# Layer two's spatial mixing: two of seven block products divided once more, their matrix sums made by DRAM transfers, and one gate a step

## The chip, the core and the metric

One core of a Trainium2 chip runs the whole program. The metric is the device time in microseconds of one execution; the kernel before took 1393.39 us (median of 3 runs, 1393.29 to 1393.97). Engines are named as the profile names them: PE (TensorE, matmuls), PEld (its weight loads), DVE (VectorE), ACT (ScalarE), POOL (GpSimd) and SP (SyncE, which only issues DMAs here).

## The reference

Four residual blocks on x, 2048 tokens by 512: linear attention, gated MLP, and both once more with the same weights. What the change touches is the gated MLP's mixing over tokens:

```python
z = _gelu(jnp.einsum("bsd,df->bsf", x, w_in))      # 2048 x 1792
z1 = z[..., :Fh]                                   # Fh = 896
z2 = _layernorm(z[..., Fh:], axis=-1)
g = jnp.einsum("ts,bsf->btf", w_sp, z2) + b_sp[None, :, None]   # w_sp: 2048 x 2048
return jnp.einsum("bsf,fd->bsd", z1 * g, w_out)
```

`w_sp` z2 is a product of 2048 x 2048 by 2048 x 896, once in each of the two layers, in float32.

## The kernel before

Every float32 matmul is made as three float32r ones: each operand is split into a high part (ScalarE copies it to float32r, `high`, L106, or L838 and L868 in the mixing) and the residual (VectorE subtracts, `low`, L109, or L839, L870 and L872), and the products high·high, high·low and low·high go to one PSUM bank (`mm3`, L120 to L122; in the mixing `acc`, L900 to L902). All engines run in the order in which the program issues their instructions; the programmer writes this order by hand.

A layer is class `P1` (attention's projections and its K-V sums, 17 steps), `transition`, class `P2` (attention's output, and the MLP's input projections; step by step for 16 tiles of 128 tokens, and with the transposed product for z1 in `f`, L673, whose GELU results go to DRAM), and class `P4`: the mixing (g = 0 to 55) and then the output projection (`o`, L988, 16 tiles of 128 tokens). During layer one's output tiles `join` (L1048) begins layer two: it loads x and weights, computes statistics and splits weights.

The mixing treats `w_sp` as 2 x 2 blocks (1024 x 1024) and z2 as 2 x 2 blocks (1024 tokens; features H1 = 0 to 383 and H2 = 512 to 895, while H3 = 384 to 511 is done in the plain way). Seven block products in the order P2, P1, P6, P7, P4, P5, P3 (`ORDER`, L808) take the place of eight. Each has 8 steps `(p, k)`, one for each 128 rows of the inner dimension. A step has six groups of three matmuls (2 row blocks of 512 tokens by three 128-feature blocks), and in P1, P2, P4 and P5 two more for H3 (`WITH3`). All matmuls are 128 x 128 by 128 x 512. P6 and P7 go on in the banks of the product before them; P2, P1 and P5 take fresh ones.

Of `w_sp`, P1, P2 and P4 read blocks of it (512 KB a step); the others read sums of blocks, made once in layer one by class `Sums` (GpSimd additions, L780, one `tick` a step) and kept in DRAM for both layers.

The loop of `P4.run` (L1013) does at iteration g: `fetch(g + 4)` (the DMA of the raw weights, issued by SP), `sp(g + 2)` (splits the weights, L838 and L839; forms the z operand, L846 to L866, and splits it, L868 to L872), `mm(g)` (the matmuls), and at a product's last step `evac` (L930: VectorE adds the bank to the result, or to the bias of the token, L937 to L960), which in four products then queues all the product's gates at once (`gate`, L924: GpSimd multiplies a 128 x 512 result by its z1 tile). z1 is loaded in one go for each of these products (`loadz1`, L907). Where P6 ends, the evacuation goes ahead of the next split, as P7 goes on in the same banks. Buffers are taken from slot lists, oldest free one first: 6 `quads` (raw weights take one, split weights one), 22 `pages`, 8 PSUM `banks`. A weight split at g thus waits for the matmuls of g - 3, and a load for the split of the raw weights three steps back.

Of the kernel before, what the change touches and what calls it, by code (L numbers as in the profile page):

```python
# [29 lines left out]
class Slots:  # L30
# [16 lines left out]
    def put(self, *tiles):  # L47
        for t in tiles:
            n, _ = self.held.pop(id(t))
            self.free_list.append(n)  # L50


@with_exitstack
def mixer_kernel(ctx: ExitStack, tc: tile.TileContext, x_in, wqkv, wo_d, win1_d, win2_d, wsp_d, bsp_d, wout_d,
# [198 lines left out]
    class P1:  # L253
# [180 lines left out]
        def run(self, sums):  # L434
            side = deque([self.win2] * NF)
            ND = NT - DEFER
            for s in range(1, NT + 2):
# [29 lines left out]
                if s == 6:  # L467
                    self.wv, self.wo = (quads.get([P, 4, 512]) for _ in range(2))
                    nc.sync.dma_start(self.wv, wqkv[:, 1024:1536].rearrange("(c p) f -> p c f", p=P))
                    nc.sync.dma_start(self.wo, wo_d.rearrange("(c p) f -> p c f", p=P))  # L470
                if s > 3 and side:
                    side.popleft().piece()
# [66 lines left out]
    class P2:  # L539
# [152 lines left out]
        def run(self, sums):  # L692
            w1 = self.win1
            for s in range(1, NT + 3):
# [52 lines left out]
                if s > 4:  # L747
                    sums.tick()
                if s >= NT + 1:
                    self.p4.fetch(s - NT - 1)  # L750
# [4 lines left out]
    class Sums:  # L755
# [3 lines left out]
        def __init__(self):  # L759
# [4 lines left out]
            self.slots = pages  # L764

        def fetch(self):
            if self.ahead:
                k, j, h = self.ahead.popleft()
                at = ((j, k), (j, k + HT), (2 + j, k)) if h == 0 else ((2 + j, k + HT),)
                self.raw.setdefault((k, j), []).extend(load(wsp_d[n, s], self.slots) for n, s in at)  # L770

# [32 lines left out]
    class P4:  # L804
# [5 lines left out]
        H1, H3, H2 = slice(0, 384), slice(384, 512), slice(512, 896)  # L810

        def __init__(self, p2, sums):
# [3 lines left out]
            self.steps = [(p, k) for p in self.ORDER for k in range(HT)]  # L816
            self.beta = self.delta = None
            self.wout = {}

        def fetch(self, g):  # L820
# [4 lines left out]
            if p in ("P1", "P2", "P4"):  # L825
# [6 lines left out]
        def sp(self, g):  # L832
            if g >= len(self.steps):
                return
            p, k = self.steps[g]
# [5 lines left out]
            self.w[g] = w  # L841
            H1, H2, H3 = self.H1, self.H2, self.H3
# [6 lines left out]
            elif p == "P1":  # L849
                z = a[:, 0:512]  # L850
                nc.vector.tensor_add(a[:, H2], a[:, H2], b[:, H2])
# [4 lines left out]
            else:  # L856
                tmp = pages.get(PAGE)
                z = tmp[:, 0:n]
                if p == "P7":
                    nc.vector.tensor_sub(z, a[:, H2], a[:, H1])  # L860
                elif p == "P4":
# [15 lines left out]

        def mm(self, g):
            p, k = self.steps[g]
            h, l = self.z.pop(g)  # L880
            w = self.w.pop(g)
            first, last = k == 0, k == HT - 1
            if p in ("P2", "P4") and first:
# [3 lines left out]
            if p in self.WITH3:  # L887
                for j in range(2):
                    self.acc(self.delta[j], h, l, self.H3, w, j, first and p in ("P2", "P4"),
# [6 lines left out]
            quads.put(w)  # L896

# [9 lines left out]
        def loadz1(self, p):  # L907
            js = range(2)
            todo = {"P1": [(2 + j, 3) for j in js] + [(2 + j, f) for j in js for f in range(3)],
                    "P4": [(j, f) for j in js for f in range(3)],  # L910
                    "P5": [(j, 3) for j in js] + [(j, 4 + f) for j in js for f in range(3)],
                    "P3": [(2 + j, 4 + f) for j in js for f in range(3)]}
            for n, f in todo.get(p, ()):
# [200 lines left out]
```

## Time and profile before

| | |
|---|---|
| median of 3 runs | 1393.39 us |
| the profiled execution | 1393.49 us |
| its span, first to last instruction | 1391.6 us |
| DVE, ACT, POOL busy in the span | 853.8, 562.1, 387.7 us |
| layer two's mixing in the span | about 1039.5 to 1311 us |

A profile has: the page (busy times, 40 slices, DMA queues, the chain that ended last, groups of instructions); lists of who waited for whom; timelines (start, duration, engine, line, operation, output and inputs; in brackets the idle time ahead and what ended it); and windows (for each stretch its length, then busy time and number of instructions of PE, PEld, DVE, ACT and POOL, the granted clock, the DMA engines' share and GB/s). A matmul's duration in it is longer than the distance to the next one's start, as matmuls overlap.

### The profile page before, as it was taken

What the parts mean: (1) busy time and instruction counts of PE and PEld (TensorE: products, weight loads), DVE (VectorE), ACT (ScalarE), POOL (GpSimd) and SP (SyncE); (2) the same over time, 40 slices, a digit from 0 to 9 for tenths busy, and PEclk for the clock granted to TensorE, in tenths of its full rate; (3) what the DMA queues carried; (4) which work ended last, traced back from release to release, by engine and by line L of the source; (5) the groups of instructions that cost most, each with busy time, mean ns of one, the idle gap of its engine ahead of it and who ended that gap; (6) DMA issues with size and microseconds to landing.
All of it is one profiled execution on the core that took longest, in us unless ns stands there. A gap on an engine that the chain in (4) does not pass through costs nothing.

```text
span 1391.6 us, 17297 instructions
## 1 busy us (share of the span) xinstructions
PE 1385.0 (100%) x6230; PEld 1158.6 (83%) x6230; DVE 853.8 (61%) x1251; ACT 562.1 (40%) x847; POOL 387.7 (28%) x490
## 2 busy tenths in 40 slices
PE   9999999999999999999999999999999999999998
PEld 7888888888888888888888888888888888888887
DVE  6665878852677766573566668766424566666632
ACT  6664533444323332341366645443343233323410
POOL 3333455544357102040023324432100030022300
PEclk9999999999999999999999999999999999999999
DMA  5541267875998533543645313555334253434432
GB/s 166 194 116 59 91 225 249 260 235 201 327 318 280 174 121 136 175 159 121 212 125 192 106 40 122 181 174 175 98 128 153 91 181 122 145 112 166 152 114 91
DMA packets 142262, 225.67 MB, mean 162 GB/s; under 512 B 11744, under 2 KB 50400, under 8 KB 142176
## 3 DMA queue, kind: packets, MB, share of 16 engines
q1 hardware_dynamic: 142176, 224.57, 49.3%
q8 instruction: 48, 0.79, 0.2%
q14 instruction: 38, 0.31, 0.1%
HBM read 156.63 MB, written 67.90 MB: 161 GB/s over the span
## 4 chain that ended last, share of the span: by engine, by line
PE 96%; DVE 2%; ACT 1%; POOL 1%; issue 0%; DMA 0%; POOLq 0%; DVEq 0%; ACTq 0%
PE bank L122 18%; PE bank L121 18%; PE bank L120 18%; PE bank L902 13%; PE bank L901 13%; PE bank L900 13%; PE bank L512 1%; PE bank L523 0%; PE bank L208 0%; DVE st L183 0%; PE bank L412 0%; DMA pg<-in_wsp_dram 0%; POOL rs L188 0%; DVE pg L109 0%; ACT pg L196 0%
## 5 line engine op out<-in xcount | busy, mean ns | idle before, releaser
L900 PE MATMUL bank<-qd,pg 128*128 128x512 f32 x800 | 311.2, 389 | 0.0
L901 PE MATMUL bank<-qd,pg 128*128 128x512 f32 x800 | 311.2, 389 | 0.0
L902 PE MATMUL bank<-qd,pg 128*128 128x512 f32 x800 | 311.2, 389 | 0.0
L839 DVE TENSOR_TENSOR qd<-qd,qd 128x1024 fp32r<-128x1024 f32 x112 | 152.8, 1365 | 175.4 <-ACT qd L838 173.2
L838 ACT ACTIVATE qd<-qd 128x1024 fp32r<-128x1024 f32 x112 | 118.5, 1058 | 215.7 <-PE bank L902 183.2
L927 POOL TENSOR_TENSOR bg<-bg,pg 128x512 f32<-128x512 f32 x56 | 85.4, 1562 | 397.0 <-DVE bg L954 188.2
L900 PEld LDWEIGHTS bank<-qd,pg 128*128 128x128 f32 x800 | 150.1, 188 | 31.4
L901 PEld LDWEIGHTS bank<-qd,pg 128*128 128x128 f32 x800 | 150.2, 188 | 31.2
L902 PEld LDWEIGHTS bank<-qd,pg 128*128 128x128 f32 x800 | 150.2, 188 | 31.0
L122 PE MATMUL bank<-qd,pg 128*128 128x512 f32 x384 | 149.7, 390 | 0.0
L187 POOL TENSOR_SCALAR rs<-mv 128x1 f32<-128x1 f32 x96 | 27.2, 284 | 352.5 <-DVE mv L185 351.8
L196 ACT ACTIVATE pg<-pg,nb,rs 128x512 f32<-128x512 f32 x63 | 51.1, 810 | 173.0 <-POOL nb L190 172.9
L120 PE MATMUL bank<-qd,pg 128*128 128x512 f32 x288 | 112.3, 390 | 0.0
L121 PE MATMUL bank<-qd,pg 128*128 128x512 f32 x288 | 112.2, 390 | 0.0
L780 POOL TENSOR_TENSOR pg<-pg,pg 128x512 f32<-128x512 f32 x64 | 94.2, 1472 | 50.7 <-DMA pg<-in_wsp_dram 27.9
L120 PE MATMUL bank<-bg,qd 128*128 128x448 f32 x256 | 94.1, 368 | 0.5 <-ACT qd L106 0.5
L121 PE MATMUL bank<-bg,qd 128*128 128x448 f32 x256 | 93.6, 366 | 0.0
L122 PE MATMUL bank<-bg,qd 128*128 128x448 f32 x256 | 93.5, 365 | 0.1
L122 PE MATMUL bank<-qd,bg 128*128 128x512 f32 x224 | 87.5, 390 | 0.0
L121 PE MATMUL bank<-qd,bg 128*128 128x512 f32 x224 | 87.4, 390 | 0.0
L120 PE MATMUL bank<-qd,bg 128*128 128x512 f32 x224 | 87.2, 389 | 0.0
L120 PE MATMUL bank<-wo,qd 128*128 128x512 f32 x224 | 87.1, 389 | 0.0
(120 smaller groups left out, 2499.9 us busy)
## 6 DMA issues: line engine op xcount, KB each, us to landing
qd<-s SPq DMA_DIRECT2D x64, 512.0 KB, 3.4
qd<-in_wsp_dram SPq DMA_DIRECT2D x48, 512.0 KB, 3.8
pg<-in_wsp_dram SPq DMA_DIRECT2D x64, 256.0 KB, 4.7
s<-pg SPq DMA_DIRECT2D x64, 256.0 KB, 4.5
pg<-x SPq DMA_DIRECT2D x64, 256.0 KB, 2.9
z<-pg SPq DMA_DIRECT2D x56, 256.0 KB, 2.8
pg<-z SPq DMA_DIRECT2D x56, 256.0 KB, 5.3
x<-pg SPq DMA_DIRECT2D x48, 256.0 KB, 2.6
```

Of the source, the lines that this page charges most:

```text
L120: nc.tensor.matmul(out, ah, bh, start=start, stop=False)
L121: nc.tensor.matmul(out, ah, bl, start=False, stop=False)
L122: nc.tensor.matmul(out, al, bh, start=False, stop=stop)
L187: nc.gpsimd.tensor_scalar(rs, mv[:, 1:2], LN_EPS, None, op0=OP.add)
L196: nc.scalar.activation(y, x, AF.Identity, bias=nb, scale=rs)
L780: nc.gpsimd.tensor_tensor(t, a, b, op=OP.add)
L838: nc.scalar.activation(w[:, 0], r, AF.Copy)
L839: nc.vector.tensor_sub(w[:, 1], r, w[:, 0].bitcast(F32))
L900: m(out, h[:, o], w[:, 0, j, :], start=start, stop=False, skip_group_check=True)
L901: m(out, h[:, o], w[:, 1, j, :], start=False, stop=False, skip_group_check=True)
L902: m(out, l[:, o], w[:, 0, j, :], start=False, stop=stop, skip_group_check=True)
L927: nc.gpsimd.tensor_tensor(u, u, z1, op=OP.mult)
```

## The change

In layer two alone the products P2 and P4 (`DIVIDED`) are each divided once more: the block product (1024 tokens of inner dimension, 512 features H1 and H3, 2 x 512 output tokens) becomes seven products r = 1 to 7, in the order 1, 5, 6, 2, 7, 3, 4 (`SEVEN`), of 512 by 256 by 512. Each has two steps q of four groups of three matmuls (two 128-row pieces by two 128-feature blocks). Their weights are blocks of `w_sp` (r = 1, 2, 4) or sums of blocks (r = 5, 6, 7, 3).

The sums are made without an engine's arithmetic (`halve`): SP copies a 512 KB block from DRAM to DRAM, and later a DMA issued by POOL adds another block onto the copy. There are 16 copies and 16 additions: for P2 at layer one's output tiles 0 to 7 (copies) and 8 to 15 (additions), for P4 in `P1.run` of layer two at steps 3 to 10 and in `P2.run` at steps 4 to 11. Two of four sums take an earlier sum as their addend. On POOL's queue, by the order of instructions, the last six additions for P2 stand directly behind one another, between the statistics that `join` asks for and the first statistics of `P1.run`.

The z operands of the divided products are made four steps ahead: `zsum` subtracts two 128 x 256 pieces (r = 5, 6, 7, 4), `zpart` splits them. For this, P1 forms a difference that P2 made before, and P7 makes in place what P4 put into temporaries. `evac_div` evacuates after the second step of each r; r = 1 goes by ScalarE into two more banks, which r = 6, 7, 4 go on in. P7's evacuation leaves a ScalarE copy of each result, on which P4's evacuations build. P1 and P5 take fresh banks for H3.

In both layers `loadz1` goes; z1 tiles are asked for three gates ahead (`ask`), and gates queue in `gq`, of which `tick` does one at each step that isn't divided and at each output tile.

```diff
+DIVIDED = ((), ("P2", "P4"))
...
+            if self.L == 1 and 3 <= s < 11:
+                sums.halve(13 + s)
...
-            if s > 4:
+            if self.L == 0 and s > 4:
...
+            if self.L == 1 and 3 < s < 12:
+                sums.halve(20 + s)
...
+        self.parts, self.halves = [], {}
+        for p in DIVIDED[1]:
+            for q in range(2):
+                for m in range(1, 5):
+                    self.halves[p, m, q] = dram.tile([2, P, 512], F32, name=f"h{p}_{m}_{q}")
+        self.parts = [(what, p, m, q) for p in DIVIDED[1] for what in ("copy", "add") for m in (1, 3, 2, 4)
+                      for q in range(2)]
...
     def fetch(self):
...
+    def halve(self, n):
+        if n >= len(self.parts):
+            return
+        what, p, m, q = self.parts[n]
+        row = 2 if p == "P2" else 0
+        j, s = {1: ((1, 0), (1, 4)), 3: ((0, 0), (1, 0)), 2: ((0, 0), None), 4: ((0, 4), None)}[m][what == "add"] or (0, 0)
+        src = wsp_d[row + j, HT + s + 2 * q:HT + s + 2 * q + 2]
+        if what == "copy":
+            nc.sync.dma_start(self.halves[p, m, q], src)
+        else:
+            if m in (2, 4):
+                src = self.halves[p, m // 2, q]
+            nc.gpsimd.dma_start(self.halves[p, m, q], src, accum_op=OP.add, max_dma_last_dim=4096)
...
     def store(self):
...
+    SEVEN = (1, 5, 6, 2, 7, 3, 4)
...
     def __init__(self, p2, sums):
...
-        self.steps = [(p, k) for p in self.ORDER for k in range(HT)]
+        self.div = DIVIDED[self.L]
+        self.steps = []
+        for p in self.ORDER:
+            if p in self.div:
+                self.steps += [(p, 2 * r + q) for r in range(7) for q in range(2)]
+            else:
+                self.steps += [(p, k) for k in range(HT)]
+        self.tmp, self.bank = {}, {}
...
+        self.asked, self.gq = deque(self.gates()), deque()
...
     def fetch(self, g):
...
-        if p in ("P1", "P2", "P4"):
+        if p in self.div:
+            r, q = self.SEVEN[k // 2], k % 2
+            j, s = {1: (0, 0), 2: (0, 4), 4: (1, 4)}.get(r, (0, 0))
+            if r in (1, 2, 4):
+                s += HT + 2 * q
+                ap = wsp_d[(2 if p == "P2" else 0) + j, s:s + 2]
+            else:
+                ap = self.sums.halves[p, {5: 1, 6: 2, 7: 3, 3: 4}[r], q]
+            nc.sync.dma_start(t, ap.rearrange("j p t -> p j t"))
+        elif p in ("P1", "P2", "P4"):
...
     def sp(self, g):
+        self.wsp(g)
+        if g < len(self.steps) and self.steps[g][0] not in self.div:
+            self.zsp(g)
+    def wsp(self, g):
...
-        p, k = self.steps[g]
...
+    def zsp(self, g):
+        p, k = self.steps[g]
...
         elif p == "P1":
...
+            if "P2" in self.div:
+                nc.vector.tensor_sub(a[:, H2], a[:, H1], a[:, H2])
...
         elif p == "P6":
...
             if p == "P7":
...
+                if "P4" in self.div:
+                    nc.vector.tensor_sub(b[:, H1], a[:, H2], b[:, H1])
+                    nc.vector.tensor_sub(b[:, H3], b[:, H3], a[:, H3])
             elif p == "P4":
...
+    def zdiv(self, half, side, q, i):
+        return ztile[HT + 4 * half + 2 * q + i][:, 256 * side:256 * side + 256]
+    def zsum(self, g):
+        if g >= len(self.steps) or self.steps[g][0] not in self.div:
+            return
+        p, m = self.steps[g]
+        r, q = self.SEVEN[m // 2], m % 2
+        if r in (1, 2, 3):
+            return
+        V, z = nc.vector, self.zdiv
+        t = self.tmp[r, q] = self.tmp[6, q] if r == 4 else pages.get([P, 2, 256])
+        for i in range(2):
+            if r == 5:
+                V.tensor_sub(t[:, i], z(0, 1, q, i), z(0, 0, q, i))
+            elif r == 6:
+                V.tensor_sub(t[:, i], z(1, 1, q, i), self.tmp[5, q][:, i])
+            elif r == 7:
+                V.tensor_sub(t[:, i], z(0, 1, q, i), z(1, 1, q, i))
+            else:
+                V.tensor_sub(t[:, i], z(1, 0, q, i), t[:, i])
+    def zpart(self, g):
+        if g >= len(self.steps) or self.steps[g][0] not in self.div:
+            return
+        p, m = self.steps[g]
+        r, q = self.SEVEN[m // 2], m % 2
+        V = nc.vector
+        h, l = pages.get([P, 2, 256], F32R), pages.get([P, 2, 256], F32R)
+        if r in (1, 2, 3):
+            half, side, sign = {1: (0, 0, 1.0), 2: (1, 0, 1.0), 3: (1, 1, -1.0)}[r]
+            for i in range(2):
+                src = self.zdiv(half, side, q, i)
+                nc.scalar.activation(h[:, i], src, AF.Copy, scale=sign)
+            for i in range(2):
+                src = self.zdiv(half, side, q, i)
+                if sign > 0:
+                    V.tensor_sub(l[:, i], src, h[:, i].bitcast(F32))
+                else:
+                    V.scalar_tensor_tensor(l[:, i], src, sign, h[:, i].bitcast(F32), op0=OP.mult,
+                                           op1=OP.subtract)
+        else:
+            split(h, l, self.tmp[r, q])
+            if r == 6:
+                pages.put(self.tmp.pop((5, q)))
+            if r in (7, 4):
+                pages.put(self.tmp.pop((r, q)))
+        self.z[g] = (h, l)
+    def mm_div(self, g, p, m):
+        r, q = self.SEVEN[m // 2], m % 2
+        h, l = self.z.pop(g)
+        w = self.w.pop(g)
+        name = "F" if r in (5, 3) else "X" if r in (1, 2) else "Y"
+        if q == 0 and r in (1, 5):
+            self.bank[name] = [banks.get(PAGE) for _ in range(2)]
+        if q == 0 and r == 6:
+            pass
+        for i in range(2):
+            for f in range(2):
+                self.acc(self.bank[name][f], h[:, i], l[:, i], slice(f * P, (f + 1) * P), w, i,
+                         r in (1, 5) and q == 0 and i == 0, r in (2, 3, 4) and q == 1 and i == 1)
+        pages.put(h, l)
+        quads.put(w)
+    def evac_div(self, p, r):
+        V, bs = nc.vector, self.bs
+        name = "F" if r in (5, 3) else "X" if r in (1, 2) else "Y"
+        if r == 1:
+            self.bank["Y"] = [banks.get(PAGE) for _ in range(2)]
+        for f in range(2):
+            bank = self.bank[name][f]
+            if r == 1:
+                nc.scalar.activation(self.bank["Y"][f], bank, AF.Copy, scale=-1.0)
+                continue
+            j, half, sign, new = {5: (1, 1, 1, True), 6: (0, 1, -1, True), 2: (0, 0, 1, True), 7: (1, 1, 1, False),
+                                  3: (0, 1, -1, False), 4: (1, 0, 1, True)}[r]
+            n, f = (2 + j if p == "P2" else j), 2 * half + f
+            if p == "P4" and f < 3:
+                sign, new = -sign, False
+            u = self.unit(n, f)
+            old = bs[n] if new else u
+            (V.tensor_add if sign > 0 else V.tensor_sub)(u, old, bank)
+        if r in (2, 3, 4):
+            banks.put(*self.bank.pop(name))
     def mm(self, g):
...
+        if p in self.div:
+            self.mm_div(g, p, k)
+            return
...
-        if p in ("P2", "P4") and first:
+        fresh = p in ("P2", "P4") or self.joins(p)
+        if fresh and first:
...
-                self.acc(self.delta[j], h, l, self.H3, w, j, first and p in ("P2", "P4"),
+                self.acc(self.delta[j], h, l, self.H3, w, j, first and fresh,
...
+    def joins(self, p):
+        return {"P1": "P2", "P5": "P4"}.get(p) in self.div
     def acc(self, out, h, l, o, w, j, start, stop):
...
     def unit(self, n, f):
...
-    def loadz1(self, p):
+    def gates(self):
...
-        todo = {"P1": [(2 + j, 3) for j in js] + [(2 + j, f) for j in js for f in range(3)],
-                "P4": [(j, f) for j in js for f in range(3)],
-                "P5": [(j, 3) for j in js] + [(j, 4 + f) for j in js for f in range(3)],
-                "P3": [(2 + j, 4 + f) for j in js for f in range(3)]}
-        for n, f in todo.get(p, ()):
-            self.z1[n, f] = load(z1s[self.L, n, f])
+        return ([(2 + j, 3) for j in js] + [(2 + j, f) for j in js for f in range(3)]
+                + [(j, f) for j in js for f in range(3)]
+                + [(j, 3) for j in js] + [(j, 4 + f) for j in js for f in range(3)]
+                + [(2 + j, 4 + f) for j in js for f in range(3)])
+    def ask(self, n):
+        while self.asked and len(self.z1) < n:
+            u = self.asked.popleft()
+            self.z1[u] = load(z1s[self.L, *u])
+    def tick(self):
+        if self.gq:
+            self.gate(*self.gq.popleft())
+            self.ask(3)
...
     def loadb(self):
...
-                V.tensor_add(self.unit(n, 3), self.delta[j], bs[n])
+                V.tensor_add(self.unit(n, 3), self.unit(n, 3) if self.joins(p) else bs[n],
+                             self.delta[j])
...
                 elif p == "P7":
...
+                    if "P4" in self.div:
+                        nc.scalar.activation(self.unit(b, f), self.unit(b, 4 + f), AF.Copy)
                 elif p == "P4":
...
-                if p in ("P2", "P4", "P3"):
+                if p in ("P2", "P4", "P3") or (p == "P7" and "P4" in self.div):
...
-        for n, f in gates:
-            self.gate(n, f)
+        self.gq.extend(gates)
...
     def wpiece(self, f):
...
+        ahead = deque()
+        if self.div:
+            self.zpart(0)
+            self.zpart(1)
+            ahead.extend([2, 3, 4, 5, 6, 7][:4 - 2])
+            self.zsum(2)
         while p2.f():
-            pass
+            if ahead:
+                g = ahead.popleft()
+                self.zsum(g + 1)
+                self.zpart(g)
+        while ahead:
+            g = ahead.popleft()
+            self.zsum(g + 1)
+            self.zpart(g)
...
+        if self.div:
+            self.loadb()
...
         for g in range(n):
...
-            if not evac_first:
+            div_first = p in self.div and k == 13 and p == "P4"
+            if not evac_first and not div_first:
...
+                self.zsum(g + 4 + 1)
+                self.zpart(g + 4)
...
-            if g == 3:
+            if g == 3 and not self.div:
...
-            if k == (6 if p == "P1" else 4):
-                self.loadz1(p)
+            if p in self.div:
+                if k % 2 == 1:
+                    self.evac_div(p, self.SEVEN[k // 2])
+                if div_first:
+                    self.sp(g + 2)
+                if k == 13 and p == "P4":
+                    self.gq.extend((n, f) for n in range(2) for f in range(3))
+                continue
+            if p == "P1" and k == 6:
+                self.ask(3)
+            self.tick()
...
+            self.tick()
...
     def join(self, i, nxt):
...
+        self.sums.halve(i)
...
```

## The prediction

> **What bounds the kernel now.** I read the page first, then who waits for whom, then the order of time around layer two's mixing. The page:
>
> ```profile
> span 1391.6 us, 17297 instructions
> PE 1385.0 (100%) x6230; PEld 1158.6 (83%) x6230; DVE 853.8 (61%) x1251; ACT 562.1 (40%) x847; POOL 387.7 (28%) x490
> PE   9999999999999999999999999999999999999998
> ...
> PEclk9999999999999999999999999999999999999999
> ```
>
> TensorE is busy all through, at the full granted clock. The list of who waited for whom, cut to TensorE, has only two rows, both at the kernel's start:
>
> ```profile
> PE bank L412 <- DVE pg L407: 2.3, 1, 2.3
> PE bank L120 <- ACT qd L106: 0.5, 1, 0.5
> ```
>
> So no other engine costs anything today; the time is the number of matmuls times their interval. That interval isn't the 389 ns that the groups give as the duration of one, because matmuls overlap. It is read from their starts. These rows of the timeline are the first step of layer two's product P2, and beside it the three operations that prepare a step on ScalarE and VectorE:
>
> ```profile
> 1039.50 0.39 PE L900 MATMUL bank<-qd,pg 128*128 128x512 f32 x1
> ...
> 1040.19 1.05 ACT L838 ACTIVATE qd<-qd 128x1024 fp32r<-128x1024 f32 x1
> ...
> 1041.28 1.23 DVE L839 TENSOR_TENSOR qd<-qd,qd 128x1024 fp32r<-128x1024 f32 x1 [10.28 <-ACT qd L838]
> ...
> 1042.22 0.39 PE L900 MATMUL bank<-qd,pg 128*128 128x512 f32 x1
> ...
> 1042.42 0.55 DVE L848 TENSOR_TENSOR z_z<-z_z 128x384 f32<-128x384 f32 x1
> ...
> 1042.89 0.69 DVE L870 TENSOR_TENSOR pg<-z_z,pg 128x512 fp32r<-128x512 f32 x1
> ```
>
> Twelve matmuls lie between 1039.50 and 1042.22: 2.72/12 = 0.227 us each. A step of P2 (24 matmuls) is 5.44 us, one of P6 or P7 (18) 4.08 us, a step of the new form (12) 2.72 us.
>
> **The change part by part.**
>
> *Matmuls.* A product of 8 steps of 24 is 192; seven half-depth products of 2 steps of 12 are 168. Twice 24 are removed, nowhere is one added: 48 x 0.227 = **10.9 us**. The order of instructions of both kernels confirms 48 fewer on TensorE.
>
> *VectorE in the divided products.* This is the step that decides. Steps halve, but each still brings a 128x1024 weight block to split. The windows of product P2 and of P7, with engines' busy times, and the rows that price the rest:
>
> ```profile
> 1039.50:1082.90 43.40, 43.40 (x193) 35.95 (x192) 22.39 (x31) 14.71 (x19) 0.00 (x0) 1.00 0.48 151
> ...
> 1159.20:1191.70 32.50, 32.50 (x145) 26.93 (x144) 21.05 (x31) 12.98 (x17) 0.00 (x0) 1.00 0.41 131
> ```
> ```profile
> 1155.98 4.09 DVE L950 TENSOR_TENSOR bg<-bank,pg 128x512 f32<-128x512 f32 x6 [0.78 <-PE bank L902]
> ...
> 1190.22 0.55 DVE L862 TENSOR_TENSOR pg<-z_z,z_z 128x384 f32<-128x384 f32 x1
> 1190.69 0.28 DVE L863 TENSOR_TENSOR pg<-z_z,z_z 128x128 f32<-128x128 f32 x1
> ...
> 1191.82 0.39 PE L900 MATMUL bank<-qd,pg 128*128 128x512 f32 x1
> ...
> 1192.29 3.67 DVE L952 TENSOR_TENSOR bg<-pg,bank 128x512 f32<-128x512 f32 x6
> ```
>
> VectorE (third pair: 22.39 of 43.40) is half idle in P2 today. From start to start an operation costs about 0.08 less than its duration: the weight residual 1.14 (1041.28 to 1042.42), the 384-wide one 0.47, six evacuations 3.6. The new 256-wide operations are in no row; between the 128-wide 0.28 and the 384-wide 0.55 lies 0.42, so 0.34 from start to start, with ends of 0.20 and 0.47. One divided product: 14 residuals x 1.14 = 16.0; 28 of 256 wide (12 residuals, 16 sums) x 0.34 = 9.5; 8 residuals of 512 x 0.61 = 4.9; 12 evacuations x 0.60 = 7.2. Sum **37.6 us, against 168 x 0.227 = 38.1 us of TensorE**. It fits by 0.5 us, so order decides. Weights are split two steps ahead and the z pieces four, and an evacuation starts when its own bank is done, before the step's last matmuls: P6's began at 1155.98, while P7's first matmul stands 8 x 4.08 ahead of P4's at 1191.82, so at 1159.2. The first four pieces of P2 are made under the preceding 1792-feature matmuls, where VectorE had the 10.28 us of idle quoted above. Laying the queues in order with these prices I find TensorE waiting at two places:
>
> - P2's second step. Its weight split comes behind the last GELU (ScalarE 1040.19), and the residual ends at 1041.28 + 1.23 = 1042.51. Today the first step hides that till 1044.9; a step of 2.72 us ends at 1042.22: **0.3 us**.
> - P4's third step. P7's six evacuations now have six ScalarE copies behind them, and that step's weight split comes behind the copies. VectorE takes up the evacuations 0.3 us before P7's last matmul (today 0.5 us after it: 1192.29, where P4 begins at 1191.82) and ends them 3.4 us after it. One copy (0.6), the split (1.05), the residual (1.23) and three handovers of 0.05 follow: 6.4 us, where the step is due after 2 x 2.72 = 5.44: **0.9 us**.
>
> P7's own steps take two more in-place subtractions (0.47 + 0.21) and, in its second half, pieces for P4: 21.05 us busy of 32.50 becomes about 31. They fit, with nothing to spare.
>
> For the 256-wide price, I add **0.5 us**: at 0.47 instead of 0.34 the divided products come to 41.3 us each, and the same walk then waits 5.2 us in all instead of 1.2. The value is near the interpolated row and keeps both ends.
>
> *Loads.* Each divided step needs 512 KB, at 2.72 us 193 GB/s.
>
> ```profile
> qd<-s SPq DMA_DIRECT2D x64, 512.0 KB, 3.4
> qd<-in_wsp_dram SPq DMA_DIRECT2D x48, 512.0 KB, 3.8
> ...
> DMA  5541267875998533543645313555334253434432
> GB/s 166 194 116 59 91 225 249 260 235 201 327 318 280 174 121 136 175 159 121 212 125 192 106 40 122 181 174 175 98 128 153 91 181 122 145 112 166 152 114 91
> ```
>
> The slice with 327 GB/s has the DMA engines 9 tenths busy, so 193 is under 6 tenths. A raw buffer comes round in three steps (8.2 us) and is held by a load (3.8), a split (1.05) and a residual (1.23): 6.1 us. **0 us**; 1 us more per load would cost about 3 us.
>
> *Copies and adding transfers.* None lies near its use: P2's are asked for while layer one's output is made (up to 700 us), P4's in layer two's first two stages, and are read after 1039 us. They cost only by what they delay. The tightest place is the end of layer one:
>
> ```profile
> 683.97 0.63 ACT L106 ACTIVATE qd<-pg 128x512 fp32r<-128x512 f32 x1 [5.20 <-DMA pg<-in_wqkv_dram]
> 685.22 0.95 ACT L106 ACTIVATE qd<-bg 128x896 fp32r<-128x896 f32 x1 [0.62 <-PE bank L122]
> ```
> ```profile
> 660.00:680.00 20.00, 20.00 (x90) 16.57 (x89) 9.99 (x15) 6.86 (x9) 3.16 (x9) 1.00 0.64 197
> 680.00:700.00 20.00, 20.00 (x90) 16.53 (x89) 11.99 (x17) 5.75 (x9) 0.00 (x0) 1.00 0.54 198
> ```
>
> ScalarE already waits there for a weight, with the split of an output tile queued behind it; that split was needed about 2.5 us after it was made, with 0.6 more of waiting for TensorE. A weight landing 5 us later (twice its time, two streams sharing engines already 0.64 and 0.54 busy) would cost some 2 us, a landing under 3 us later nothing. I take 0, end 3. GpSimd's issue of a transfer is in no row; near its other instructions (0.2 to 1.3 us) it disappears in GpSimd's idle 72%.
>
> The Trainium skill speaks against this part in "SBUF — State Buffer", section "SBUF: two separate sides": descriptors of a GpSimd-issued DMA are made by GpSimd's own cores and starve while VectorE holds the shared port. No trace of before has such a DMA. By that rule the adds land late and GpSimd is held longer, which only the third rival would pay for.
>
> *Gates one a step, in both layers.* They move GpSimd work that no TensorE wait names. What they can cost is VectorE time:
>
> ```profile
> 1130.84 1.65 DVE L872 SCALAR_TENSOR_TENSOR pg<-z_z,pg 128x384 fp32r<-128x384 f32 x1
> ...
> 1138.44 0.55 DVE L872 SCALAR_TENSOR_TENSOR pg<-z_z,pg 128x384 fp32r<-128x384 f32 x1
> ```
>
> The first ran beside eight gates in a row, the second after them: one gate delays one VectorE operation by 1.1 us. Spread out, that is 1.1 us per step of 4.08 or 5.44 us, in steps that have 1 to 2 us free; none falls in a divided product. Each z1 load is asked three gates ahead, and the last six gates come with the first six output tiles, where the tiles that need them are split from the seventh on. **0 us**, end 1.
>
> *Sum.* The profiled run took 1393.5 (span 1391.6 and 1.9 around it), 0.1 above the median of three. 1393.5 - 10.9 + 0.3 + 0.9 + 0.5 = **1384.3 us**.
>
> **The rivals.**
>
> *VectorE becomes the bound of the divided products.* For it: 37.6 of 38.1 us. Against: two to four steps of lead. With a 256-wide operation at the 384-wide end, 0.47, the walk loses 5.2 us: 1393.5 - 10.9 + 5.2 = 1388 us.
>
> *The loads become the bound.* For it: 193 GB/s steadily, beside four broadcast loads of 256 KB at P2's start. Against: DMA stays under 6 tenths busy by the same slices. At 1 us more each the walk loses 4.2 in all: 1387 us.
>
> *Slower: the adding transfers hold GpSimd over the layer boundary.* All eight for P2 stand on GpSimd's queue after its last work in layer one, and the fifth to eighth wait for the first to sixth to land (each sum is built on an earlier one). Behind them stands layer two's first statistics:
>
> ```profile
> 703.09 0.22 POOL L187 TENSOR_SCALAR rs<-mv 128x1 f32<-128x1 f32 x1 [27.90 <-DVE mv L185]
> ...
> 711.29 0.22 POOL L187 TENSOR_SCALAR rs<-mv 128x1 f32<-128x1 f32 x1 [6.96 <-DVE mv L185]
> ```
>
> They are tied to normalisations one step (8.2 us) ahead of use. The second add goes out about 675, so six of them, 3.1 MB, have until 711: it decides when adds run below 3.1 MB / 36 us = 87 GB/s together. At 60 GB/s they end at 727, 16 us late: 1384.3 + 16, some 1400 us; at half the threshold 1420. Copies at 3.8 us per 512 KB (138 GB/s, one at a time) speak against it; that an add has two operands to fetch speaks for it. The Trainium skill, "Collectives: The Full Stack", section "The bandwidth ceiling: the fold count and why AG ≠ RS ≠ AR", says that a transfer that adds runs at half the rate of a copy for its second read; with the 327 GB/s of the slices that is an estimate of 163 GB/s, over the threshold, and no run here shows it yet.
>
> **How the numbers follow.** Forecast (1382.5 to 1386.5): 0.55, at 1384.3. VectorE bound: 0.15, at 1388. Loads: 0.08, at 1387. Slower by held GpSimd: 0.15, at 1400. The same mechanism, half as strong, eating just about the gain: 0.07, at 1393. A measurement of this kernel can tell about 0.2% (2.8 us) from no change, so faster means under 1390.6: 0.55 + 0.15 + 0.08 = 0.78; same 0.07; slower 0.15. The range is 1382.5 (all 10.9 kept) to 1391.0.
>
> **What would show it.** TensorE has 48 matmuls fewer, still 0.227 us apart. In P2 and P4 of layer two VectorE is over 0.9 busy, and TensorE's waits name L839's successor there, 1 to 2 us in all; rather 5 us, over many even steps, if VectorE is the bound, and a wait of ScalarE's split for a DMA if the loads are. Before 711 us GpSimd's first statistics of layer two are on time. If TensorE waits long in layer two's first stage, behind statistics, the third rival holds; if it waits at the layer boundary behind weight loads, I mis-sized the contention.

## The result, and the profile after

| kernel | median (range, runs) | against before, 95% interval |
|---|---|---|
| before | 1393.34 us (1392.18 to 1393.97, 4 runs) | |
| after | 1404.71 us (1402.34 to 1405.76, 4 runs) | 1.008 [1.0063, 1.0098] |

The change makes the kernel 0.8% slower; forecast were 1384.3 us and a gain. The 48 matmuls are gone and the mixing is shorter, but elsewhere more is lost. First the page of the kernel after: busy times, slices of TensorE and of its clock, and the DMA queues (packets, MB, share of 16 engines' span).

```profile
span 1402.1 us, 17453 instructions
PE 1380.4 (98%) x6182; PEld 1150.6 (82%) x6182; DVE 889.9 (63%) x1331; ACT 587.1 (42%) x893; POOL 398.8 (28%) x506
PE   9999999999999999999799999999999999999998
...
PEclk9999999999999999999899999999999999999999
...
q1 hardware_dynamic: 145952, 239.26, 51.3%
q0 software_dynamic: 2304, 8.39, 3.5%
```

One slice of 35 us, the twentieth, has TensorE at 7 and its clock at 8 tenths: 666 to 701 us. That is layer one's end, not the mixing, which begins at 1056. Queue q0, new, is the GpSimd-issued adding transfers. The list of who waited for whom in the kernel after, cut to TensorE (us in total, times, longest):

```profile
PE bank L125 <- DVE qd L112: 9.6, 2, 8.8
PE bank L123 <- ACT qd L109: 3.0, 2, 2.7
PE bank L415 <- DVE pg L410: 2.3, 1, 2.3
PE bank L1056 <- DVE qd L890: 1.5, 3, 0.8
PE bank L1055 <- ACT qd L889: 0.7, 1, 0.7
```

L415 is the old wait at the start. L1055 and L1056 are the mixing. L123 and L125 are everything else, and the two long ones among them are in these windows of the kernel after (length, busy time of PE, PEld, DVE, ACT, POOL, granted clock, DMA share, GB/s):

```profile
660.00:680.00 20.00, 20.00 (x90) 16.55 (x89) 9.39 (x14) 4.97 (x6) 8.43 (x15) 1.00 0.88 224
680.00:700.00 20.00, 11.20 (x42) 8.82 (x41) 2.98 (x4) 2.11 (x3) 1.65 (x3) 0.74 1.07 261
700.00:720.00 20.00, 16.59 (x65) 12.98 (x64) 11.71 (x18) 7.10 (x12) 0.20 (x1) 0.91 0.56 196
```

From 680 to 720 TensorE is busy 27.79 of 40 us and idle for 12.2. VectorE and ScalarE are emptier than before, but the DMA engines are at 0.88 and then full (1.07, which reads as 1) in the first two windows, where before had 0.64 and 0.54. What fills them is in the DMA part of the page for 665 to 705 us (queues; then transfers, KB each, median us from issue to landing), before and then after:

```profile
q1 hardware_dynamic: 5472, 7.87, 58.2%
...
pg<-x SPq DMA_DIRECT2D x8, 256.0 KB, 5.2
...
pg<-in_wqkv_dram SPq DMA_DIRECT2D x8, 256.0 KB, 5.3
```
```profile
q0 software_dynamic: 1152, 4.19, 57.7%
q1 hardware_dynamic: 4399, 5.89, 42.1%
...
hP<-in_wsp_dram POOLq DMA_DIRECT2D x4, 512.0 KB, 8.5
pg<-in_wqkv_dram SPq DMA_DIRECT2D x8, 256.0 KB, 11.9
hP<-hP POOLq DMA_DIRECT2D x4, 512.0 KB, 11.1
pg<-x SPq DMA_DIRECT2D x6, 256.0 KB, 12.9
```

The eight adds for P2 take 57.7% of 40 us, 23.1 us of all 16 engines. The program's own transfers needed 58.2% there, 23.3 us. 46.4 us of transfers do not fit in 40, so 1.98 MB of the program's own (7.87 - 5.89) slid out of the stretch, and TensorE waited for them.

Now in order of time. GpSimd's timeline of the kernel after gives the adds' issue; here the first, the sixth and the eighth, and the next statistic behind them:

```profile
665.65 1.06 POOL L799 DMA_DIRECT2D hP<-in_wsp_dram  x1
...
679.24 0.81 POOL L799 DMA_DIRECT2D hP<-hP  x1 [0.98 <-DMA hP<-in_wsp_dram]
...
693.58 0.81 POOL L799 DMA_DIRECT2D hP<-hP  x1 [1.97 <-DMA hP<-hP]
719.80 0.23 POOL L190 TENSOR_SCALAR rs<-mv 128x1 f32<-128x1 f32 x1 [25.42 <-DVE mv L188]
```

Six go out within 14 us (665.65 to 679.24), the last three of them far ahead of the output tiles they were written beside, because nothing on GpSimd's queue makes an add wait for its tile. GpSimd is free again at 694.4, and the next statistic on its queue, at 719.80, waits for VectorE's `mv`, not for an add. Then SyncE's timeline of the kernel after (issue time and its length), VectorE's, and TensorE's:

```profile
674.56 0.69 SPq L100 DMA_DIRECT2D pg<-x  x1
...
686.99 7.02 SPq L100 DMA_DIRECT2D pg<-in_wqkv_dram  x4
```
```profile
693.13 0.69 DVE L1163 TENSOR_TENSOR pg<-pg,bank 128x512 f32<-128x512 f32 x1 [11.15 <-DMA pg<-x]
693.73 1.08 DVE L112 TENSOR_TENSOR qd<-bg,qd 128x896 fp32r<-128x896 f32 x1
```
```profile
685.68 0.39 PE L124 MATMUL bank<-wo,qd 128*128 128x512 f32 x1
694.87 0.80 PE L125 MATMUL bank<-wo,qd 128*128 128x512 f32 x1 [8.80 <-DVE qd L112]
695.47 0.63 PE L123 MATMUL bank<-wo,qd 128*128 128x512 f32 x1
695.89 0.63 PE L124 MATMUL bank<-wo,qd 128*128 128x512 f32 x1
696.32 0.63 PE L125 MATMUL bank<-wo,qd 128*128 128x512 f32 x1
```

One load of x, 256 KB, lands 18.5 us after its issue (the longest of that tile's; 674.56 + 18.5 = 693.06). VectorE's residual addition for an output tile waits for it. Behind that on VectorE's queue stands the residual split of the next output tile, and TensorE needs that split: 8.80 us of idle at a place where no load is an operand of the matmul. The second wait runs through ScalarE. The next four weights were issued 8.4 us later than before (686.99 in the SyncE row; in before's timeline 678.60), and the issue itself took 7.02 us (before 2.27). ScalarE's timeline of the kernel after:

```profile
702.24 0.63 ACT L109 ACTIVATE qd<-pg 128x512 fp32r<-128x512 f32 x1 [17.85 <-DMA pg<-in_wqkv_dram]
702.77 0.93 ACT L109 ACTIVATE qd<-bg 128x896 fp32r<-128x896 f32 x1
```

Its output split (702.77) stands behind the weight's (702.24), and TensorE waits 2.7 us more.

The rest is the clock. In the long wait it falls to half, and it falls again behind the second; windows of the kernel after:

```profile
688.00:690.00 2.00, 0.00 (x0) 0.00 (x0) 0.00 (x0) 0.00 (x0) 0.00 (x0) 0.53 1.09 238
...
696.00:698.00 2.00, 2.00 (x6) 1.54 (x5) 0.00 (x0) 0.00 (x0) 0.00 (x0) 0.50 1.05 238
...
706.00:708.00 2.00, 2.00 (x7) 1.54 (x6) 2.00 (x4) 1.15 (x3) 0.00 (x0) 0.50 0.83 306
```

The matmuls from 695.47 lie 0.427 us apart (695.47, 695.89, 696.32) and not 0.227. From 679.79 to 715.78 there are 88 matmul starts; 87 x 0.2267 = 19.7 us, the stretch took 36.0, so **16.3 us** are lost at the layer boundary. From start to start, 12.8 of them are waiting (9.0, 2.8, and 1.0 in two pieces) and 3.4 slow clock; the windows' 12.2 is a little less, as they count a matmul's whole duration as busy. The Trainium skill, "TensorE: Matmul & The Clock Gate", section "Part 1: The HAM clock gate (the "warmup" mystery)", says that an idle window of some 3.4 us drops the clock to half and that about as long under load is needed to get it back. On the return this trace agrees (half clock from 694.87 to 698.4, and 1.00 behind it). The drop came sooner than after 3.4 us of idling: the last matmul ended at 686.07 (685.68 + 0.39), and the 0.53 of the window from 688 to 690 puts the half clock at 688.1, 2.0 us later.

The balance in span: -10.9 (matmuls) + 16.3 (boundary) + 4.35 (waits in the mixing) + 0.7 (the remainder, elsewhere) = +10.5, from 1391.6 to 1402.1.

The waits in the mixing come from matmul starts. Divided P2 takes 40.40 us for 168 matmuls (38.09 at 0.2267): 2.31 lost. P4 takes 39.73: 1.64 lost. P5 loses 0.4 at its start, the other products nothing. P2's loss is mostly one place, timeline of the kernel after:

```profile
1057.94 1.92 SPq L1086 DMA_DIRECT2D pg<-in_bsp_dram  x4
...
1059.95 2.02 SPq L871 DMA_DIRECT2D qd<-hP  x2
```
```profile
1067.09 1.06 ACT L889 ACTIVATE qd<-qd 128x1024 fp32r<-128x1024 f32 x1 [2.40 <-DMA qd<-hP]
1067.13 0.39 PE L1057 MATMUL bank<-qd,pg 128*128 128x512 f32 x1
...
1068.18 1.23 DVE L890 TENSOR_TENSOR qd<-qd,qd 128x1024 fp32r<-128x1024 f32 x1 [3.11 <-ACT qd L889]
1068.20 0.50 PE L1055 MATMUL bank<-qd,pg 128*128 128x512 f32 x1 [0.69 <-ACT qd L889]
...
1069.32 0.75 DVE L976 TENSOR_TENSOR pg<-z_z,pg 128x256 fp32r<-128x256 f32 x2
```

The fifth step's weights are asked for behind four bias loads of 256 KB. Their split waits 2.40 us for them, and matmuls that should follow 1067.13 by 0.23 follow by 1.07, and once more by 1.26 for the residual (1069.46). The last row is the price that no row had: two 256-wide operations in 0.75 us, so 0.34 from start to start and 0.41 long.

### The profile page after: what moved, and what is told of

The parts are those of the page before. It is cut to its first block, busy times and chain, and to the rows that moved or that the text cites. A ratio compares the mean times of both kernels' runs of the same rounds, so it can differ in the third digit from the quotient of the medians.

```text
span 1402.1 us, 17453 instructions
## 1 busy us (share of the span) xinstructions
PE 1380.4 (98%) x6182; PEld 1150.6 (82%) x6182; DVE 889.9 (63%) x1331; ACT 587.1 (42%) x893; POOL 398.8 (28%) x506
## 3 DMA queue, kind: packets, MB, share of 16 engines
q1 hardware_dynamic: 145952, 239.26, 51.3%
q0 software_dynamic: 2304, 8.39, 3.5%
## 4 chain that ended last, share of the span: by engine, by line
PE 88%; DVE 4%; DMA 3%; ACT 2%; issue 1%; POOL 1%; SPq 1%; ACTq 0%; DVEq 0%; POOLq 0%
PE bank L125 17%; PE bank L123 17%; PE bank L124 17%; PE bank L1056 12%; PE bank L1057 12%; PE bank L1055 12%; DMA pg<-in_wqkv_dram 2%; DVE qd L890 1%; DVE st L186 1%; PE bank L517 1%; DMA qd<-hP 1%; PE bank L528 0%; DMA pg<-in_x_dram 0%; SPq L100 0%; ACT qd L889 0%
## 5 line engine op out<-in xcount | busy, mean ns | idle before, releaser
L1056 PE MATMUL bank<-qd,pg 128*128 128x512 f32 x784 | 305.6, 390 | 1.5 <-DVE qd L890 1.5
L1055 PE MATMUL bank<-qd,pg 128*128 128x512 f32 x784 | 305.3, 389 | 0.7 <-ACT qd L889 0.7
L1057 PE MATMUL bank<-qd,pg 128*128 128x512 f32 x784 | 305.2, 389 | 0.0
L890 DVE TENSOR_TENSOR qd<-qd,qd 128x1024 fp32r<-128x1024 f32 x124 | 168.9, 1363 | 137.1 <-ACT qd L889 137.0
L889 ACT ACTIVATE qd<-qd 128x1024 fp32r<-128x1024 f32 x124 | 131.1, 1057 | 191.9 <-PE bank L1057 151.7
L1056 PEld LDWEIGHTS bank<-qd,pg 128*128 128x128 f32 x784 | 147.2, 188 | 33.9 <-DVE qd L890 3.4
L1055 PEld LDWEIGHTS bank<-qd,pg 128*128 128x128 f32 x784 | 147.2, 188 | 32.0 <-ACT qd L889 1.1
L1057 PEld LDWEIGHTS bank<-qd,pg 128*128 128x128 f32 x784 | 147.2, 188 | 30.8 <-DVE pg L929 0.4
L125 PE MATMUL bank<-qd,pg 128*128 128x512 f32 x384 | 149.7, 390 | 0.0
L123 PE MATMUL bank<-qd,pg 128*128 128x512 f32 x288 | 112.5, 391 | 0.3 <-DVE pg L112 0.2
L124 PE MATMUL bank<-qd,pg 128*128 128x512 f32 x288 | 112.3, 390 | 0.2 <-DVE qd L112 0.2
L125 PE MATMUL bank<-wo,qd 128*128 128x512 f32 x224 | 89.0, 397 | 9.6 <-DVE qd L112 9.6
L123 PE MATMUL bank<-bg,qd 128*128 128x448 f32 x256 | 94.2, 368 | 0.4 <-ACT qd L109 0.4
L125 PE MATMUL bank<-bg,qd 128*128 128x448 f32 x256 | 93.6, 365 | 0.1
L123 PE MATMUL bank<-wo,qd 128*128 128x512 f32 x224 | 88.5, 395 | 2.7 <-ACT qd L109 2.7
L124 PE MATMUL bank<-wo,qd 128*128 128x512 f32 x224 | 88.1, 393 | 0.0
L125 PE MATMUL bank<-qd,bg 128*128 128x512 f32 x224 | 87.5, 390 | 0.0
```

The costliest lines, as they stand in the source:

```text
L123: nc.tensor.matmul(out, ah, bh, start=start, stop=False)
L124: nc.tensor.matmul(out, ah, bl, start=False, stop=False)
L125: nc.tensor.matmul(out, al, bh, start=False, stop=stop)
L889: nc.scalar.activation(w[:, 0], r, AF.Copy)
L890: nc.vector.tensor_sub(w[:, 1], r, w[:, 0].bitcast(F32))
L1055: m(out, h[:, o], w[:, 0, j, :], start=start, stop=False, skip_group_check=True)
```

## The experiments

The theory after the result: the eight adds, bunched, fill the DMA engines at the boundary (A). Rivals: a transfer that adds is bad wherever it stands, by something other than its engine time (B); the divided products, or the gates, cost what is missing and the boundary would be late anyway (C). Each kernel below is the kernel after with the edit shown, unless another is named.

**1. The adds spread over layer two.** Copies for P2 stay in layer one; all 16 adds move, eight in `P1.run` (every second step) and the others in `P2.run`, one a step, with the copies for P4 as well.

```diff
-                if self.L == 1 and 3 <= s < 11:
-                    sums.halve(13 + s)
+                if self.L == 1 and s % 2 == 0 and 2 <= s < 17:
+                    sums.halve(7 + s // 2)
...
-                if self.L == 1 and 3 < s < 12:
-                    sums.halve(20 + s)
+                if self.L == 1 and s < 17:
+                    sums.halve(15 + s)
...
-            self.sums.halve(i)
+            if i < 8:
+                self.sums.halve(i)
```

> The same 16 copies and 16 adding transfers, at other places: P2's adds one at every second step of layer two's first stage (steps 2 to 16) in place of output tiles 8 to 15 of layer one; P4's copies and adds one a step in the second stage. Theory A (eight adds bunched at the layer boundary take the DMA engines from the x and weight loads there, which costs 16 us; the mixing itself keeps 10.9 - 4.4 = 6.5 us): 1386 to 1388 us, and TensorE's waits between 680 and 710 us are gone. Rival B (an add hurts wherever it runs, as loads are due everywhere): 1393 or more, with waits in layer two's first stage. Rival C (the loss at the boundary comes from the gates done one at each output tile): 1403, the waits stay.

Measured: 1387.62 us (1386.74 to 1389.08, 4 runs), ratio 0.9957 [0.9942, 0.9972]. The same adds, as many and as large (8.39 MB, 3.8% of the 16 engines), now cost nothing at the boundary; the window of this kernel:

```profile
680.00:700.00 20.00, 20.00 (x90) 16.57 (x89) 11.57 (x16) 5.74 (x9) 0.00 (x0) 1.00 0.60 211
```

TensorE is busy throughout, the DMA engines 0.60. The mixing still loses 4.1 us (P2 2.03, P4 1.64, P5 0.4). A holds as to place; B as it was put falls.

**2. No copies and no adds.** This kernel leaves the sums out: it reads plain blocks of `w_sp` where the sums belong, with as much to load.

```diff
-                if self.L == 1 and 3 <= s < 11:
-                    sums.halve(13 + s)
...
-                if self.L == 1 and 3 < s < 12:
-                    sums.halve(20 + s)
...
-                    ap = self.sums.halves[p, {5: 1, 6: 2, 7: 3, 3: 4}[r], q]
+                    ap = wsp_d[(2 if p == "P2" else 0) + (r in (5, 7)), HT + 2 * q:HT + 2 * q + 2]
...
-            self.sums.halve(i)
```

> All copies and adds are left out; the divided products read plain blocks of the same size in place of the sums (so the mixing of layer two computes something else). What is left is the divided mixing and the gates. Theory A: 1386 to 1388, equal to the run with the adds apart within 1 us. If the copies issued by SP also cost, this is faster than the run with the adds apart by what they cost. Rival C: 1403.

Measured: 1386.62 us (1386.05 to 1387.16, 4 runs), 0.9949 [0.9934, 0.9963]. Without any sums P2 still loses 2.28, P4 1.62 and P5 0.42, so these waits have nothing to do with the adds. The 1.0 us to the first experiment is inside the two intervals: that spread adds cost anything is not shown.

**3. The gates alone.** Nothing is divided.

```diff
-DIVIDED = ((), ("P2", "P4"))
+DIVIDED = ((), ())
```

> No product is divided, so no sums either; only the gates one a step and their z1 loads three ahead are left of the change, in both layers. Theory A: 1393.4 within 0.7 us. Rival C: some 16 us slower, 1409, with TensorE's waits at the layer boundary.

Measured: 1394.15 us (1393.25 to 1394.84, 10 runs), 1.0003 [0.9993, 1.0012]. One gate a step and z1 asked for three ahead cost nothing that can be measured. With the second experiment, C falls: the divided products keep most of the gain, and the gates take none.

**4. Copies where the adds are.** The same 16 transfers at the same places, but copying; this kernel leaves the additions out.

```diff
-                nc.gpsimd.dma_start(self.halves[p, m, q], src, accum_op=OP.add, max_dma_last_dim=4096)
+                nc.gpsimd.dma_start(self.halves[p, m, q], src, max_dma_last_dim=4096)
```

> Every adding transfer becomes a plain copy of the same block, issued by GpSimd at the same place (so the sums are not formed, and layer two's mixing computes something else). Theory A in the form that the adding counts (an add took 23 us of all 16 engines for eight, 2.9 us each, against 1.5 for 512 KB at the rate of the copies): engine time at the boundary falls by 11 us and the wait mostly goes: 1387 to 1393. If it is any transfer issued by GpSimd, or its bytes, that holds the loads: 1400 or more.

Measured: 1390.82 us (1388.96 to 1392.05, 8 runs), 0.9977 [0.9967, 0.9988]. The page and two windows of this kernel:

```profile
q0 software_dynamic: 2304, 8.39, 1.9%
```
```profile
680.00:700.00 20.00, 17.88 (x72) 13.96 (x71) 8.94 (x13) 4.91 (x8) 1.03 (x2) 0.91 0.95 359
...
694.00:696.00 2.00, 2.00 (x7) 1.51 (x6) 1.14 (x3) 1.41 (x3) 0.00 (x0) 0.50 1.04 402
```

The same bytes on the same queue at the same moment take 1.9% of 1389.9 us, 26.4 us of the 16 engines, where the adds take 3.5% of 1402.1, 49.1 us: 1.65 us a transfer and 3.07. TensorE is idle 2.1 us in this stretch and not 8.8; with a short drop of the clock, 4.3 us are lost there by matmul starts, where the kernel after lost 16.3. So what an add costs matters, and not the bunch alone: about half the engine time at the same place cuts 13.9 us of the 17.1 between the kernel after and the first experiment. Whether it is the engine time of an add that does the harm, or something else in which it differs from a copy, this run does not separate.

**5. The adds one behind each output tile.** Adds where the change put them, but each held back by a small GpSimd instruction that reads the finished output tile, so that they go out at the tiles' pace.

```diff
             nc.vector.tensor_add(x, x, b)
+            if self.L == 0 and i >= 8:
+                pace = small.tile([P, 1], F32, name="pace")
+                nc.gpsimd.tensor_scalar(pace, x[:, 0:1], LN_EPS, None, op0=OP.add)
```

> P2's eight adds stay at layer one's output tiles 8 to 15, but each now follows a tiny GpSimd operation that reads that tile's residual sum, so they go out one a tile (4.8 us apart) instead of six in 14 us. If the bunch alone is the harm: within 2 us of the run with the adds apart, 1387 to 1390. If it is the engine time (eight adds of 2.9 us beside loads that already take 0.54 to 0.64 of the engines make 47 us of work in 38 us): still 4 to 12 us lost at the boundary, 1391 to 1400.

Measured: 1390.3 us (1389.44 to 1394.23, 10 runs), 0.998 [0.9971, 0.9989]. The eight adds go out over 38 us (667.8 to 705.5) and not 28. The window of this kernel:

```profile
680.00:700.00 20.00, 17.76 (x77) 14.09 (x76) 11.08 (x16) 6.91 (x11) 5.99 (x7) 1.00 1.06 329
```

The DMA engines are still full, but TensorE is idle 2.2 us and keeps its clock; 2.9 us are lost by matmul starts. Pacing alone thus takes back about 14 of the 17 us, as the cheaper transfers of experiment 4 did at the old pace: the two shares overlap and cannot be added. The time lies between the two that were expected, so neither the bunch nor the engine time is the whole cause. The landings go with it: asked for from 665 to 705 us, loads of x land after 7.8 us median and weights after 7.8 (7.6 and 8.5 in experiment 4), where the kernel after has 12.9 and 11.9 and before 5.2 and 5.3.

**6. On the first experiment: raw weights and biases asked for earlier in the mixing's preparation.**

```diff
             self.sp(0)
             ahead = deque()
             if self.div:
+                self.wsp(1)
+                self.fetch(3)
+                self.loadb()
...
-            self.sp(1)
-            self.fetch(3)
-            if self.div:
-                self.loadb()
+            if not self.div:
+                self.sp(1)
+                self.fetch(3)
```

> The run with the adds apart, and ahead of the last z1 products the split of the second weight block, the fourth raw load and the four bias loads (which stood behind them, in front of the fifth and sixth raw load). Theory: of the 2.0 us lost in P2, 0.2 at its second step come from the late split, 1.7 at its fifth step from the raw load behind 1 MB of bias loads; both go, 1385.6 (2.0 less than with the adds apart). Rival (VectorE's load of 37.6 of 38.1 us is what stops P2): no change, 1387.6, the same gaps.

Measured: 1384.98 us (1383.98 to 1385.84, 5 runs), 0.9936 [0.9923, 0.9948]. P2 now takes 38.08 us: nothing is lost in it, neither at the second step nor at the fifth. The edit moves a split, a raw load and the bias loads together; which of them gave how much no run separates. P4 (1.64) and P5 (0.40) stand as they were. Of the mixing, TensorE's wait list in this kernel has one row left, P4's (in the first experiment it stood at 1.5, with 0.4 at L1055):

```profile
PE bank L1056 <- DVE qd L890: 0.7, 2, 0.4
```

**7. On the first experiment: the six ScalarE copies after P7 made one a step in P4.**

```diff
-                        if "P4" in self.div:
-                            nc.scalar.activation(self.unit(b, f), self.unit(b, 4 + f), AF.Copy)
...
+                if p in self.div and p == "P4" and 2 <= k < 8:
+                    j, f = ((1, 2), (0, 2), (0, 0), (0, 1), (1, 0), (1, 1))[k - 2]
+                    nc.scalar.activation(self.unit(j, f), self.unit(j, 4 + f), AF.Copy)
```

> The run with the adds apart, and the six ScalarE copies behind P7's evacuation go one a step into P4's steps 2 to 7, behind that step's splits. Theory: the 0.7 us lost at P4's third step go, 1386.9. Rival (the evacuations themselves are late on VectorE): no change.

Measured: 1385.54 us (1384.77 to 1386.8, 5 runs), 0.9941 [0.9929, 0.9954]. P4 loses 0.18 in place of 1.64: with the wait at its third step, the small ones late in P4 are gone too. P2 loses 1.5, P5 0.43.

**8. Both of them on the first experiment.**

> Both edits on the run with the adds apart. If the two losses are independent: 2.7 us less than with the adds apart, 1384.9, which would be 8.5 us or 0.6% under the kernel before; what is left of the 10.9 us is then some 1 us at the end of P4.

Measured: 1383.67 us (1382.79 to 1384.03, 5 runs), 0.9926 [0.9912, 0.9939], faster than both kernels. Its span and the windows of the divided P2 and P4:

```profile
span 1382.1 us, 17453 instructions
```
```profile
1040.00:1078.10 38.10, 38.10 (x169) 31.53 (x168) 33.64 (x52) 23.36 (x33) 0.00 (x0) 1.00 0.75 235
1186.90:1225.20 38.30, 38.30 (x170) 31.30 (x168) 37.12 (x56) 24.14 (x37) 4.82 (x3) 1.00 0.61 179
```

9.5 us of the 10.9 arrive in the span, with VectorE busy 37.12 of 38.30 us in P4 and TensorE busy in all of both windows.

## Why the prediction was wrong

**Matmuls: right.** 6182 for 6230, 0.227 us apart; P2 with nothing lost takes 38.08 us (experiments 6 and 8), as 168 x 0.2267.

**VectorE in the divided products: right.** The 256-wide price came out at the interpolated 0.34, VectorE is busy 37.1 us in P4's window (experiment 8) where 37.6 were worked out, and the products still run at TensorE's pace. In P2's it is busy 33.6 of 38.1, 0.88 and not over 0.9, as P2's first pieces are made ahead of it. P7's load, put at about 31 us, is 28.0 in the kernel after. The 0.5 us added for the unknown price was not needed. At the second step of P2 the walk said 0.3, measured 0.2. At P4's third step it said 0.9:

```profile
1205.08 3.67 DVE L1119 TENSOR_TENSOR bg<-pg,bank 128x512 f32<-128x512 f32 x6
...
1210.40 1.23 DVE L890 TENSOR_TENSOR qd<-qd,qd 128x1024 fp32r<-128x1024 f32 x1 [1.65 <-ACT qd L889]
```
```profile
1211.68 0.50 PE L1056 MATMUL bank<-qd,pg 128*128 128x512 f32 x1 [0.44 <-DVE qd L890]
```

Evacuations, then the copies on ScalarE, then split and residual, and the matmul at 1211.68, 0.6 late, and 0.1 behind it: 0.7 measured, by the chain described, and experiment 7 removes it. Not foreseen were about 0.9 us of small waits late in P4, gone with the same edit (how the moved copies caused them I did not follow), and 0.4 at P5's start, where no run tried anything.

**Loads, "0 us": too low by about 2 us, at one place.** I had named the four broadcast loads at P2's start under the loads rival and judged them by the mean of slices. What counts is order: SyncE's queue puts 1 MB of biases ahead of a raw weight that has steps of 2.72 us to arrive in. Experiment 6 takes 2.0 us out of P2 by order alone (the split's and the loads'), the 0.2 of its second step among them. The rival itself, loads late at every step, did not come.

**Copies and adding transfers, "I take 0, end 3": the step that failed; it was 16.3 us.** I priced one weight landing 5 us late. The term should have been a sum of engine time: eight adds at 2.9 to 3.1 us are 23 to 25 us of all 16 engines, and the windows that I quoted (0.64 and 0.54 busy) had only about 16 us free in 40. I took an add to be like a copy in its effect on others and weighed its rate in the rival alone, against 87 GB/s. And I followed one consumer, the weight split on ScalarE. The larger wait came by a load of x whose consumer on VectorE stands ahead of a split that TensorE needs; each of these is plain in the program's order. The last 3.4 us, the halved clock, no step held.

The sentence that would have shown it was in the prediction ("if it waits at the layer boundary behind weight loads, I mis-sized the contention"); the term was not carried to the range, which ended at 1391.0.

The Trainium skill's page "Collectives: The Full Stack", section "The bandwidth ceiling: the fold count and why AG ≠ RS ≠ AR", puts an adding transfer at half a copy's rate, and the prediction made an estimate of 163 GB/s of it. This trace agrees: 8.39 MB in 49.1 us is 171 GB/s, the hardware queue's 239.26 MB in 51.3% of 1402.1 us 333 GB/s. The rule spoke against the change, and I asked it only the one question.

**Gates, "0 us": right.** Experiment 3: +0.03%, interval -0.07 to +0.12%.

**The rivals.** VectorE as the bound: no. Adds that hold GpSimd over the boundary: the sign and, within 5 us, the time were that rival's (1400), the mechanism was not. GpSimd was free at 694.4, and its next statistic waited for VectorE. 4.19 MB in the 40 us from 665 to 705 are 105 GB/s, and the 87 it needed are fewer. The adds do land late (8.5 and 11.1 us median; the eight for P4, spread thinly in layer two, 7.6 and 8.0). The Trainium skill's "SBUF — State Buffer", section "SBUF: two separate sides", would have that come from VectorE, which starves GpSimd's descriptors while it runs an operation that takes both ports; but VectorE stood idle for 11.15 us in the middle of the bunch, and the DMA engines were full. No run separates the two.

**What stays open:** why SyncE's issue of four weights took 7.02 us in place of 2.27 (full queues are the obvious reading, not shown); whether spread adds cost up to 1 us; and whether an add harms its neighbours by its longer engine time alone.

## What to carry to other kernels

Price a background transfer as engine time, add it to the busy share of the very stretch in which its queue will let it run, and if the sum is over one, follow each load of that stretch to what is queued behind its consumer on that engine. A transfer that is not due for 350 us still has to be paced, by a wait of its own or by steps that have room; the place in the program's text paces nothing. When a product's steps become shorter, look again at everything that is queued ahead of its first loads.

## What the runs showed of the hardware

- A DMA that adds DRAM to DRAM took 3.07 us of all 16 engines for 512 KB (3.29 in experiment 1), the copy from the same queue 1.65.
- Beside the bunched adds, loads of 256 KB landed after 12.9 us median and 18.5 at the longest, before 5.2 median.
- A wait of 9.0 us cost TensorE another 1.7 us at half clock, and one of 2.8 us with 1.0 behind it 1.7 us again (0.50 in 706 to 708).
- The length of a single wait does not tell whether the clock falls. It fell in experiment 4 behind waits of 1.37 and 0.75 us (0.50 in 694 to 696) and stayed at 1.00 in experiment 5 over one of 1.97. In these traces the changes of the granted clock lie whole multiples of 3.41 us apart (688.11, 698.35, 705.17 and 708.59 in the kernel after). Counted in such stretches, TensorE was idle 2.0 and 2.7 us in those at whose ends the clock fell in the kernel after, and 2.1 in experiment 4's. In experiment 5 the long wait lay across an end, with 1.1 us before it and 0.9 behind. That the idle share of such a stretch decides is a reading of these few cases; no run was made to test it.
